# q and k of batches 1 to 7 transposed by DMA instead of by TensorE, in attention followed by a gated MLP

## The chip, the cores and the metric

The kernel runs on one core of one Trainium2 chip. The metric is the device time of one execution in microseconds, as a median of three runs. A core has five engines, each with its own instruction stream: TensorE (PE in the profile; its weight loads are PEld), VectorE (DVE), ScalarE (ACT), GpSimd (POOL) and SyncE (SP), which here only issues DMAs. Streams meet in semaphores. TensorE writes its results to PSUM, from which VectorE or ScalarE move them to SBUF. DMA transfers run on 16 DMA engines that all queues share.

## The reference

Eight batches, 16 query heads, 4 key/value heads, 384 positions, head size 64. Attention without a mask, then a gated MLP with a spatial mix over the positions:

```python
k = np.repeat(k, group, axis=1)              # group = 4
v = np.repeat(v, group, axis=1)
scores = scale * np.matmul(q, k.transpose(0, 1, 3, 2))
scores = scores - np.max(scores, axis=-1, keepdims=True)
attn = np.exp(scores)
attn = attn / (np.sum(attn, axis=-1, keepdims=True) + 1e-09)
x = np.matmul(attn, v)                        # then [B, S, 16 * 64] = [8, 384, 1024]

h = np.maximum(x @ w_in, 0.0)                 # [8, 384, 1024]
u, v = h[..., :512], h[..., 512:]
v_n = (v - mean(v)) / np.sqrt(var(v) + 1e-06)
v_s = np.einsum('ts,bsd->btd', w_spatial, v_n) + b_spatial[None, :, None]
out = (u * v_s) @ w_out                       # [8, 384, 1024], float32
```

Inputs and output are float32 in HBM. The kernel multiplies in fp16.

## The kernel before

**Layout.** A score matmul needs the head dimension on the partitions, for q and for k. HBM holds positions as rows, so q and k are loaded with 128 positions on the partitions (position 3p + t lies on partition p as piece t of three), cast to fp16, and transposed in blocks of 128x128: 128 positions by two heads of 64. A batch has 6 blocks of k (two pairs of heads, `gp`, times three pieces) and 24 of q (two `gp`, four heads `j` of a group, three pieces; the two heads of a block belong to the two kv heads of the pair). TensorE transposes them against an identity matrix into PSUM and VectorE copies them to SBUF: `transpose_k` makes one group of six blocks (PSUM tile `pk`, copied to `kT`), `transpose_q` one group of six (PSUM tile `pq_<gp>_<jp>`, copied to half of `qT_<gp>`). That is five groups a batch.

**Units of work.** A batch of attention has 18 score units (`scores`): two matmuls into a PSUM tile `sc` of two banks, of which there are two, and one exponential on ScalarE of 128x1024 into `aT`. Each `values` step (four a batch) runs 36 matmuls: sums of the exponentials (`sums`), of which ScalarE makes reciprocals by Ln and Exp (`rec`), and the products with v (`X`), which VectorE scales into `xT`. The MLP of a batch is a list of pieces: three `mk_v` (PSUM `pv`), four `mk_u` (`pu`), four `mk_sp` (`psp`) and six `mk_out` (`po`), with the layer norm on VectorE and ScalarE between. `sums`, `X`, `pv`, `pu`, `psp`, `po`, `pk`, `pq` and `psw` (the transposed spatial weights) share four PSUM buffers in turn, each of one bank.

**Order.** The streams of TensorE, GpSimd and SP stand in the order in which the program issues them; VectorE's and ScalarE's are scheduled by the compiler. A batch has nine visits of two score units. Behind the scores of a visit come, by visit: a `values` step (visits 0, 3, 5, 8; the one of visit 0 belongs to the batch before), a transpose group, and pieces of the MLP of the batch before, taken from a queue as long as the running sum of estimated times (`done`) is below a budget. The budget of a visit is a ninth of all estimates of a batch; a transpose group counts 0.36, and each piece its number in `feed_forward`. Transpose groups stand in visits 1 and 2 (second half of this batch's q: `pq_1_0`, `pq_1_1`) and 6, 7, 8 (next batch's k, first half of its q: `pk`, `pq_0_0`, `pq_0_1`). In batch 0 no MLP piece runs.

**Loads.** `load_batch(b + 1)` is called in visit 2 of batch b: k, first half of q, v, second half of q, all from SP into single float32 buffers, cast on GpSimd (for batch 1 k and the first half of q on VectorE). Output stores go through SP as well, one for each third of the positions (`osb`, three buffers). The MLP's weights are loaded and cast by DMAs that GpSimd issues in batch 0; the spatial weights (`ws`) come over SP.

Of the kernel before, what the change touches and what calls it, by code (L numbers as in the profile page):

```python
# [11 lines left out]
FP16 = mybir.dt.float16  # L12
# [6 lines left out]
def kernel(  # L19
# [19 lines left out]
    nc = tc.nc  # L39
    P = 128  # L40

    B, HQ, S, D = q.shape
    HKV = k.shape[1]
    G = HQ // HKV
# [3 lines left out]
    NST = S // P  # L48
    NKT = DM // P
    NDT = DH // P  # L50
    NGP = HKV // 2
# [10 lines left out]
    qk16 = ctx.enter_context(tc.tile_pool(name="qk16", bufs=2))  # L62
    tr_sb = ctx.enter_context(tc.tile_pool(name="tr_sb", bufs=3))
# [13 lines left out]
    for i, (_nm, funcs) in enumerate(get_activation_tables(nc.m.arch).items()):  # L77
        if need_funcs.issubset(funcs):
# [5 lines left out]
            name=nc.get_next_instruction_name(), act_func_set_id=set_id, ins=[], outs=[]  # L84
# [16 lines left out]
    def load_q(b, gp, pieces=1):  # L101
        q32 = ld.tile([P, 2 * G, NST * D], FP32, name=f"q32_{b}_{gp}", tag=f"q32_{gp}")
        n = 2 * G // pieces
        for i in range(pieces):
            h0 = gp * 2 * G + i * n
            nc.sync.dma_start(
                q32[:, i * n : (i + 1) * n, :],
                q[b, h0 : h0 + n].rearrange("h (p t) d -> p h (t d)", t=NST),
            )
        loaded["q32", b, gp] = q32  # L110

    def cast_k(b, engine):
        k16 = qk16.tile([P, NST, HKV, D], FP16, name=f"k16_{b}", tag="k16")
        engine.tensor_copy(k16, loaded["k32", b].rearrange("p g (t d) -> p t g d", t=NST))  # L114
        loaded["k16", b] = k16

    def cast_v(b, engine):
# [2 lines left out]
        loaded["v16", b] = v16  # L120

    def cast_q(b, gp, engine):
        q16 = qk16.tile([P, NST, G, 2, D], FP16, name=f"q16_{b}_{gp}", tag=f"q16_{gp}")
        q32 = loaded["q32", b, gp]
        for half in range(2):
            engine.tensor_copy(
                q16[:, :, :, half, :],
                q32[:, half * G : (half + 1) * G, :].rearrange("p j (t d) -> p t j d", t=NST),
            )
        loaded["q16", b, gp] = q16  # L130

# [82 lines left out]

    kT, qT, aT, xT = {}, {}, {}, {}

    def transpose_k(b):
        k16 = loaded[("k16", b)]
        pk = ps.tile([P, NGP, NST, P], FP16, name=f"pk_{b}", tag="ps")
        for gp in range(NGP):  # L220
            for t in range(NST):
                nc.tensor.transpose(  # L222
                    pk[:, gp, t, :],
                    k16[:, t, 2 * gp : 2 * gp + 2, :].rearrange("p g d -> p (g d)"),
                    ident16,
                )
        kT[b] = tr_sb.tile([P, NGP, NST, P], FP16, name=f"kT_{b}", tag="kT")
        nc.vector.tensor_copy(kT[b], pk)

    def transpose_q(b, gp, jp):  # L230
        q16 = loaded[("q16", b, gp)]
        if jp == 0:
            qT[b, gp] = tr_sb.tile([P, G, NST, P], FP16, name=f"qT_{b}_{gp}", tag=f"qT_{gp}", bufs=2)
        pq = ps.tile([P, 2, NST, P], FP16, name=f"pq_{b}_{gp}_{jp}", tag="ps")
        for jj in range(2):
            for t in range(NST):
                nc.tensor.transpose(
                    pq[:, jj, t, :],
                    q16[:, t, 2 * jp + jj, :, :].rearrange("p h d -> p (h d)"),
                    ident16,  # L240
                )
        nc.vector.tensor_copy(qT[b, gp][:, 2 * jp : 2 * jp + 2, :, :], pq)
# [169 lines left out]

    VISITS = 9
    VALUES_AT = {0: (-1, 1, 1), 3: (0, 0, 0), 5: (0, 0, 1), 8: (0, 1, 0)}
    T_SCORE, T_VALUES, T_TRANS = 0.62, 1.55, 0.36

    queue = []
    done = 0.0

    load_consts()  # L420
    with tc.manual_schedule(engines={PE, POOL, SP}):
        load_k(0)
        load_q(0, 0, pieces=2)
        cast_k(0, nc.vector)
        cast_q(0, 0, nc.vector)
        load_v(0)
        load_q(0, 1, pieces=2)
        cast_v(0, nc.gpsimd)
        cast_q(0, 1, nc.gpsimd)
        load_w_in(DH, DFF)  # L430
        load_w_in(0, DH)
        load_w_out()
        transpose_k(0)
        transpose_q(0, 0, 0)
        transpose_q(0, 0, 1)

        total = sum(t for t, _ in feed_forward(0))
        per_visit = (total + 4 * T_VALUES + 5 * T_TRANS) / VISITS
        budget = 0.0
        for b in range(B + 1):  # L440
            for vi in range(VISITS if b < B else 1):
                if b < B:
                    scores(b, [2 * vi, 2 * vi + 1])
                if vi in VALUES_AT:
                    db, gp, quad = VALUES_AT[vi]
                    if 0 <= b + db < B and (b < B or db < 0):
                        values(b + db, gp, quad)
                        done += T_VALUES
                if b < B:
                    if vi in (1, 2):  # L450
                        transpose_q(b, 1, vi - 1)
# [24 lines left out]
                if not queue:  # L476
                    done = max(done, budget - per_visit)
# [30 lines left out]
```

## Time and profile before

| | |
|---|---|
| median of 3 runs | 302.69 us (301.97 to 303.99) |
| the profiled execution | 303.19 us, span 301.4 us |
| TensorE busy | 269.2 us, 89% of the span, 2457 matmuls |
| ScalarE busy | 184.3 us, 61% |
| VectorE busy | 161.7 us, 54% |
| GpSimd busy | 53.2 us, 18% |
| mean granted TensorE clock | 0.980 |
| DMA | 35.57 MB in 31852 packets |

The profile is of one execution. Times are microseconds from the start of the span. A row of a timeline gives start, length, engine, line of the program, operation, output <- inputs, sizes and count, and in brackets how long the engine had been idle before it and what ended the wait. TensorE's matmuls overlap, so the length of a row is longer than the time by which it holds up the next one; differences of starts give that time. Tile names end in a running number of the program, which differs between the two kernels. The page leaves out the DMAs' issue from an engine's busy time; rows named SPq are issues on SP's queue.

### The profile page before, as it was taken

To read this page: it belongs to the slowest core of one execution; us is meant where nothing else is said; L and a number is where in the kernel's file an instruction comes from. 1 tells how busy PE (TensorE), PEld (TensorE's weight loads), DVE (VectorE), ACT (ScalarE), POOL (GpSimd) and SP (SyncE) were. 2 spreads that over 40 slices of the span, in tenths; PEclk is the share of its full clock that TensorE was granted. 3 is DMA by queue.
4 is the path that set the end of the run, shared out by engine and by line. 5 is a ranking of instruction groups with operands and counts; after the bars stand their busy time and mean duration, and the time that the engine had idled before them with its cause. 6 is when DMAs were issued, how large, how long until landed. Compare 5 with 4: busy or idle time off the path is not lost.

```text
span 301.4 us, 5836 instructions
## 1 busy us (share of the span) xinstructions
PE 269.2 (89%) x2457; PEld 125.4 (42%) x2457; DVE 161.7 (54%) x310; ACT 184.3 (61%) x249; POOL 53.2 (18%) x82
## 2 busy tenths in 40 slices
PE   0576879899899989999899989999899989999993
PEld 0332434444445434444345434444344434444551
DVE  3437325564465554665455654755455754645574
ACT  1396965657776585566786485566876485675300
POOL 0666952000140003200050001500051000000000
PEclk9977979999999999999999999999999999999998
DMA  7999991003660219103570219103480111003105
GB/s 216 315 287 218 116 254 35 2 0 142 197 188 2 119 52 318 37 0 141 164 222 0 103 50 316 56 2 140 137 251 0 70 73 72 0 2 139 72 0 209
DMA packets 31852, 35.57 MB, mean 118 GB/s; under 512 B 1489, under 2 KB 28114, under 8 KB 31826
## 3 DMA queue, kind: packets, MB, share of 16 engines
q1 hardware_dynamic: 28722, 32.05, 32.4%
q0 software_dynamic: 3104, 3.15, 6.8%
q8 instruction: 19, 0.31, 0.4%
q14 instruction: 7, 0.06, 0.1%
HBM read 25.76 MB, written 12.58 MB: 127 GB/s over the span
## 4 chain that ended last, share of the span: by engine, by line
PE 69%; ACT 16%; DMA 6%; DVE 4%; issue 2%; SPq 1%; POOL 0%; DVEq 0%
DMA ws_316<-in_moe_w_spatial_dram 3%; DMA q_0_1_135<-in_q_dram 3%; ACT aT_1_720 L265 1%; ACT aT_0_2385 L265 1%; ACT aT_0_969 L265 1%; ACT aT_1_335 L265 1%; ACT aT_0_1441 L265 1%; ACT aT_0_489 L265 1%; PE pv_0_588 L311 1%; ACT aT_0_3329 L265 1%; ACT aT_0_1913 L265 1%; ACT aT_0_2857 L265 1%; ACT aT_1_2613 L265 1%; ACT aT_1_3539 L265 1%; ACT aT_1_3085 L265 1%
## 5 line engine op out<-in xcount | busy, mean ns | idle before, releaser
L348 PEld LDWEIGHTS <-w_in_107 128*128 128x128 f16 x256 | 23.9, 98 | 21.6 <-issue 6.9
L186 POOL DMA_DIRECT2D w_in_107<-in_moe_w_in_dram x32 | 17.1, 543 | 5.3 <-DMA w_in_107<-in_moe_w_in_dram 5.3
L280 PEld LDWEIGHTS <-ones_103 128*32 128x32 f16 x384 | 7.4, 96 | 15.1 <-issue 13.3
L222 PE MATMUL pk_177<-ident_102,k_0_128 128*128 128x128 f16 x6 | 0.8, 303 | 9.6 <-DVE ident_102 L155 9.6
L265 ACT ACTIVATE aT_0_209<-sc_0_203 128x1024 f16<-128x1024 f32 x1 | 1.0, 1024 | 10.3 <-PE sc_0_203 L252 10.3
L114 POOL CAST k_3_1060<-k_3_1056 128x768 f16<-128x768 f32 x1 | 0.8, 827 | 33.0 <-DVE stats_0_1086 L321 33.0
L252 PEld LDWEIGHTS <-kT_184 64*128 64x128 f16 x36 | 2.1, 99 | 9.4 <-issue 8.9
L114 POOL CAST k_6_2476<-k_6_2472 128x768 f16<-128x768 f32 x1 | 0.8, 827 | 27.7 <-DMA k_6_2472<-in_k_dram 27.7
L114 POOL CAST k_5_2004<-k_5_2000 128x768 f16<-128x768 f32 x1 | 0.8, 827 | 26.6 <-DMA k_5_2000<-in_k_dram 26.6
L114 POOL CAST k_7_2948<-k_7_2944 128x768 f16<-128x768 f32 x1 | 0.8, 827 | 25.4 <-DMA k_7_2944<-in_k_dram 25.4
L114 POOL CAST k_4_1532<-k_4_1528 128x768 f16<-128x768 f32 x1 | 0.8, 827 | 25.1 <-DMA k_4_1528<-in_k_dram 25.1
L280 PEld LDWEIGHTS <-v_0_138 128*32 128x32 f16 x96 | 2.9, 106 | 4.4 <-issue 3.2
L202 DVE CAST ws_318<-ws_316 128x384 f16<-128x384 f32 x3 | 1.9, 671 | 5.2 <-DMA ws_316<-in_moe_w_spatial_dram 5.2
L222 PEld LDWEIGHTS <-k_0_128 128*128 128x128 f16 x6 | 0.6, 133 | 9.5 <-DVE k_0_128 L114 5.2
L364 PEld LDWEIGHTS <-bias_ones 128*128 128x128 f16 x32 | 3.1, 97 | 3.5 <-issue 2.3
L311 PEld LDWEIGHTS <-xt_271 128*128 128x128 f16 x24 | 2.7, 116 | 3.5 <-issue 1.6
L387 PEld LDWEIGHTS <-gT_3623 128*128 128x128 f16 x24 | 2.2, 98 | 3.5 <-issue 0.7
L387 PEld LDWEIGHTS <-gT_3895 128*128 128x128 f16 x24 | 2.3, 98 | 3.0 <-DVE gT_3895 L373 0.5
L387 PEld LDWEIGHTS <-gT_2697 128*128 128x128 f16 x24 | 2.2, 97 | 3.0 <-DVE gT_2697 L373 0.6
L387 PEld LDWEIGHTS <-gT_1753 128*128 128x128 f16 x24 | 2.2, 97 | 3.0 <-DVE gT_1753 L373 0.6
L387 PEld LDWEIGHTS <-gT_2225 128*128 128x128 f16 x24 | 2.2, 97 | 3.0 <-DVE gT_2225 L373 0.6
L387 PEld LDWEIGHTS <-gT_1281 128*128 128x128 f16 x24 | 2.2, 97 | 3.0 <-DVE gT_1281 L373 0.6
(1168 smaller groups left out, 804.7 us busy)
## 6 DMA issues: line engine op xcount, KB each, us to landing
w_in_107<-in_moe_w_in_dram POOLq DMA_DIRECT2D x32, 64.0 KB, 5.4
w_out_108<-in_moe_w_out_dram POOLq DMA_DIRECT2D x2, 512.0 KB, 7.4
q_0_0_125<-in_q_dram SPq DMA_DIRECT2D x2, 384.0 KB, 5.4
q_0_1_135<-in_q_dram SPq DMA_DIRECT2D x2, 384.0 KB, 8.3
q_1_0_247<-in_q_dram SPq DMA_DIRECT2D x1, 768.0 KB, 6.2
q_1_1_256<-in_q_dram SPq DMA_DIRECT2D x1, 768.0 KB, 8.5
q_2_0_571<-in_q_dram SPq DMA_DIRECT2D x1, 768.0 KB, 12.9
q_2_1_580<-in_q_dram SPq DMA_DIRECT2D x1, 768.0 KB, 8.2
```

Source lines behind the costliest of these rows:

```text
L114: engine.tensor_copy(k16, loaded["k32", b].rearrange("p g (t d) -> p t g d", t=NST))
L186: nc.gpsimd.dma_start(w_in16[32 * i : 32 * (i + 1), kc : kc + 2, c0:c1], rows[jq])
L202: nc.vector.tensor_copy(ws16[:, tt, :, :], ws32[:, tt, :].rearrange("p (s t) -> p t s", t=NST))
L222: nc.tensor.transpose(pk[:, gp, t, :], k16[:, t, 2 * gp : 2 * gp + 2, :].rearrange("p g d -> p (g d)"), ident16,)
L252: nc.tensor.matmul(sc[:, half, :], kT[b][lo:hi, gp, t, :], rhs[lo:hi, c * 512 : (c + 1) * 512], start=True, stop=True,)
L265: nc.scalar.activation(aT[b, gp][:, t, :, c * 512 : (c + 1) * 512], sc, AF.Exp, scale=scale)
L280: nc.tensor.matmul(dst[32 * i : 32 * (i + 1), 0:S], weights(t, half), a[:, t, half, j * S : (j + 1) * S], start=(t == 0), stop=(t == NST - 1),
L311: nc.tensor.matmul(pv, xt[:, kc, st * P : (st + 1) * P], w_in16[:, kc, DH:DFF], start=(kc == 0), stop=(kc == NKT - 1),)
L348: nc.tensor.matmul(pu[:, 0:S], w_in16[:, kc, mu * P : (mu + 1) * P], xT[b][:, kc, :], start=(kc == 0), stop=(kc == NKT - 1),)
L364: nc.tensor.matmul(psp[:, 0:S], bias_ones, bias_rows, start=True, stop=False)
L387: nc.tensor.matmul(po, gT[:, m, tt * P : (tt + 1) * P], w_out16[:, m, half * 512 : (half + 1) * 512], start=(m == 0), stop=(m == NDT - 1),)
```

## The change

The five TensorE groups stay for batch 0 alone. For each later batch three DMA transposes, issued on SP, move the fp16 tiles from SBUF to SBUF: all six blocks of k (`dma_transpose_k`), then twelve blocks of q, twice (`dma_transpose_q`). They write `kT` and `qT` directly, with no PSUM tile and no copy on VectorE. Batch b + 1's k and first half of q are issued in visit 6 of batch b, its second half of q in visit 8. The fp16 tiles get the layout in which the columns of a block lie side by side, so k is cast in two instructions of half the size. The estimate `T_TRANS` is gone from the budget, so the MLP's pieces fall on other visits.

```diff
     def cast_k(b, engine):
-        k16 = qk16.tile([P, NST, HKV, D], FP16, name=f"k16_{b}", tag="k16")
-        engine.tensor_copy(k16, loaded["k32", b].rearrange("p g (t d) -> p t g d", t=NST))
+        k16 = qk16.tile([P, NGP, NST, 2, D], FP16, name=f"k16_{b}", tag="k16")
+        k32 = loaded["k32", b].rearrange("p (gp h) (t d) -> p gp t h d", gp=NGP, t=NST)
+        for gp in range(NGP):
+            engine.tensor_copy(k16[:, gp], k32[:, gp])
...
+    def dma_transpose_k(b):
+        kT[b] = tr_sb.tile([P, NGP, NST, P], FP16, name=f"kT_{b}", tag="kT")
+        nc.sync.dma_start_transpose(
+            kT[b].rearrange("p g t q -> p (g t) q"),
+            loaded["k16", b].rearrange("p g t h d -> p (g t h d)"),
+        )
+
+    def dma_transpose_q(b, gp):
+        qT[b, gp] = tr_sb.tile([P, G, NST, P], FP16, name=f"qT_{b}_{gp}", tag=f"qT_{gp}", bufs=2)
+        nc.sync.dma_start_transpose(
+            qT[b, gp].rearrange("p j t q -> p (j t) q"),
+            loaded["q16", b, gp].rearrange("p j t h d -> p (j t h d)"),
+        )
...
-        per_visit = (total + 4 * T_VALUES + 5 * T_TRANS) / VISITS
+        per_visit = (total + 4 * T_VALUES) / VISITS
...
-                    if vi in (1, 2):
+                    if b == 0 and vi in (1, 2):
                         transpose_q(b, 1, vi - 1)
-                        done += T_TRANS
...
-                    if vi >= 6 and b + 1 < B:
-                        if vi == 6:
-                            transpose_k(b + 1)
-                        else:
-                            transpose_q(b + 1, 0, vi - 7)
-                        done += T_TRANS
+                    if vi == 6 and b + 1 < B:
+                        dma_transpose_k(b + 1)
+                        dma_transpose_q(b + 1, 0)
+                    if vi == 8 and b + 1 < B:
+                        dma_transpose_q(b + 1, 1)
```

How the order changes is shown at two places, for a batch in the middle. First SP's stream, from the loads of batch 4 to the loads of batch 5. Before:

```order
L93 DMA k_4_1528<-in_k_dram 128x4x192 [waits DMAHW3_49,DMAHW2_49,Pool_49]
L106 DMA q_4_0_1530<-in_q_dram 128x8x192 [waits DMAHW4_49,Pool_49]
L98 DMA v_4_1537<-in_v_dram 128x4x192 [waits DMAHW5_49,Pool_49]
L106 DMA q_4_1_1539<-in_q_dram 128x8x192 [waits DMAHW6_49,Pool_49]
L396 DMA out_dram<-osb_0_1795 128x1024 [waits DVE_49]
L396 DMA out_dram<-osb_1_1826 128x1024 [waits DMAHW7_49,DVE_49]
L396 DMA out_dram<-osb_2_1900 128x1024 [waits DMAHW0_49,DVE_49]
L93 DMA k_5_2000<-in_k_dram 128x4x192 [waits DMAHW2_49,DMAHW1_49,Pool_49]
```

And now:

```order
L93 DMA k_4_1421<-in_k_dram 128x4x192 [waits DMAHW3_49]
L106 DMA q_4_0_1423<-in_q_dram 128x8x192 [waits DMAHW4_49]
L98 DMA v_4_1431<-in_v_dram 128x4x192 [waits DMAHW5_49]
L106 DMA q_4_1_1433<-in_q_dram 128x8x192 [waits DMAHW6_49]
L221 DMA_TRANSPOSE kT_1655<-k_4_1425 128x6x128 [waits DMAHW7_49,Pool_49]
L228 DMA_TRANSPOSE qT_0_1657<-q_4_0_1428 128x12x128 [waits DMAHW0_49,PE_49,Pool_49]
L412 DMA out_dram<-osb_0_1692 128x1024 [waits DMAHW1_49,DVE_49]
L228 DMA_TRANSPOSE qT_1_1765<-q_4_1_1437 128x12x128 [waits DMAHW2_49,PE_49,Pool_49]
L412 DMA out_dram<-osb_1_1706 128x1024 [waits DMAHW3_49,DVE_49]
L412 DMA out_dram<-osb_2_1827 128x1024 [waits DMAHW4_49,DVE_49]
```

The two first transposes stand between the loads and the first output store, the third between the first store and the second. Each waits for a cast on GpSimd and for the DMA eight places earlier on SP (DMAHW).

Second VectorE's stream, where its rows show in which order TensorE's groups are drained from the last pieces of one batch to the layer norm in the next. Before:

```order
L394 COPY osb_1_1826<-po_1_0_1827 128x512 [waits DMAHW0_49,PE_49]
L394 COPY osb_1_1826<-po_1_1_1833 128x512 [waits PE_49]
L296 TENSOR_TENSOR xt_1606<-X_1_0_0_1864,rec_1_0_1861 128x384 [waits PE_49,Activation_49]
L296 TENSOR_TENSOR xt_1606<-X_1_0_1_1878,rec_1_0_1861 128x384 [waits PE_49]
L242 COPY qT_0_1810<-pq_0_1_1892 128x768 [waits PE_49]
L394 COPY osb_2_1900<-po_2_0_1901 128x512 [waits DMAHW1_49,PE_49]
L296 TENSOR_TENSOR xt_1606<-X_1_1_0_1932,rec_1_1_1929 128x384 [waits PE_49,Activation_49]
L296 TENSOR_TENSOR xt_1606<-X_1_1_1_1946,rec_1_1_1929 128x384 [waits PE_49]
L394 COPY osb_2_1900<-po_2_1_1960 128x512 [waits PE_49]
L242 COPY qT_1_1975<-pq_1_0_1976 128x768 [waits PE_49]
L242 COPY qT_1_1975<-pq_1_1_1992 128x768 [waits PE_49]
L321 BN_STATS stats_0_2030<-v_r_0_2028 128x6 [waits Activation_49]
```

And now:

```order
L410 COPY osb_1_1706<-po_1_0_1707 128x512 [waits DMAHW1_49,PE_49]
L312 TENSOR_TENSOR xt_1500<-X_1_0_0_1737,rec_1_0_1734 128x384 [waits PE_49,Activation_49]
L312 TENSOR_TENSOR xt_1500<-X_1_0_1_1751,rec_1_0_1734 128x384 [waits PE_49]
L410 COPY osb_1_1706<-po_1_1_1767 128x512 [waits PE_49]
L312 TENSOR_TENSOR xt_1500<-X_1_1_0_1799,rec_1_1_1796 128x384 [waits PE_49,Activation_49]
L312 TENSOR_TENSOR xt_1500<-X_1_1_1_1813,rec_1_1_1796 128x384 [waits PE_49]
L410 COPY osb_2_1827<-po_2_0_1828 128x512 [waits DMAHW2_49,PE_49]
L410 COPY osb_2_1827<-po_2_1_1834 128x512 [waits PE_49]
L337 BN_STATS stats_0_1888<-v_r_0_1886 128x6 [waits Activation_49]
```

The three `qT` copies and their TensorE groups are gone, and the output pieces moved: `po_1_1` now stands where `pq_0_1` stood, and `po_2_0` and `po_2_1` both follow the `values` step of the next batch's visit 0.

More of the change, by code (lines that the diff above doesn't have):

```diff
@@ L122, in cast_q @@
     def cast_q(b, gp, engine):
-        q16 = qk16.tile([P, NST, G, 2, D], FP16, name=f"q16_{b}_{gp}", tag=f"q16_{gp}")
+        q16 = qk16.tile([P, G, NST, 2, D], FP16, name=f"q16_{b}_{gp}", tag=f"q16_{gp}")
         q32 = loaded["q32", b, gp]
@@ L127, in cast_q @@
                 q16[:, :, :, half, :],
-                q32[:, half * G : (half + 1) * G, :].rearrange("p j (t d) -> p t j d", t=NST),
+                q32[:, half * G : (half + 1) * G, :].rearrange("p j (t d) -> p j t d", t=NST),
             )
@@ L223, in transpose_k @@
                     pk[:, gp, t, :],
-                    k16[:, t, 2 * gp : 2 * gp + 2, :].rearrange("p g d -> p (g d)"),
+                    k16[:, gp, t, :, :].rearrange("p h d -> p (h d)"),
                     ident16,
@@ L238, in transpose_q @@
                     pq[:, jj, t, :],
-                    q16[:, t, 2 * jp + jj, :, :].rearrange("p h d -> p (h d)"),
+                    q16[:, 2 * jp + jj, t, :, :].rearrange("p h d -> p (h d)"),
                     ident16,
@@ L414 @@
     VALUES_AT = {0: (-1, 1, 1), 3: (0, 0, 0), 5: (0, 0, 1), 8: (0, 1, 0)}
-    T_SCORE, T_VALUES, T_TRANS = 0.62, 1.55, 0.36
+    T_VALUES = 1.55
     queue = []
```

## The prediction

> **What bounds the kernel now.** I read the page's head first, then the busy time by stage, then TensorE's timeline across one boundary between batches, and last the DMA queues.
>
> The first fence is the page: span, TensorE's row, and the chain of work that ended last by engine.
>
> ```profile
> span 301.4 us, 5836 instructions
> PE 269.2 (89%) x2457; PEld 125.4 (42%) x2457; DVE 161.7 (54%) x310; ACT 184.3 (61%) x249; POOL 53.2 (18%) x82
> PE 69%; ACT 16%; DMA 6%; DVE 4%; issue 2%; SPq 1%; POOL 0%; DVEq 0%
> ```
>
> The second is busy time by stage: start and end, length, then each engine's busy time, granted clock, DMA share and GB/s.
>
> ```profile
> 12.00:30.00 18.00, 12.10 (x120) 4.88 (x117) 9.40 (x16) 14.21 (x18) 12.61 (x24) 0.82 1.09 268
> 30.00:42.00 12.00, 9.44 (x119) 4.68 (x119) 4.72 (x9) 11.88 (x15) 11.31 (x18) 0.93 1.00 147
> 113.00:147.30 34.30, 32.90 (x308) 15.15 (x306) 18.95 (x36) 22.91 (x33) 5.00 (x6) 1.00 0.36 117
> ```
>
> In the steady stage (113 to 147.3 us is one batch) TensorE is busy 32.9 of 34.3 us, ScalarE 22.9, VectorE 19.0, at a granted clock of 1.00; the DMA engines are in use for 0.36 of it, 12.3 us. So TensorE's instruction stream sets the batch time, and what leaves that stream shortens it, except where TensorE then waits for ScalarE. Before 42 us it is different: the DMA engines are full (shares 1.09 and 1.00), and ScalarE is busy 11.9 of 12 us.
>
> TensorE's timeline (start us, length us, instruction) shows both kinds of place. First the end of one batch and the start of the next; then the same places around batch 7, behind which no batch follows.
>
> ```profile
> 112.86 1.89 PE L311 MATMUL pv_0_1547<-w_in_107,xt_1134 128*128 128x512 f16 x8
> 137.70 0.67 PE L280 MATMUL sums_1_0_1848<-aT_1_1669,ones_103 128*32 128x384 f16 x12
> 139.28 0.51 PE L237 MATMUL pq_0_1_1892<-ident_102,q_4_0_1534 128*128 128x128 f16 x6
> 139.97 1.02 PE L387 MATMUL po_2_0_1901<-w_out_108,gT_1753 128*128 128x512 f16 x4 [0.18 <-ACT rec_1_0_1861 L291]
> 140.93 0.39 PE L252 MATMUL sc_0_1907<-qT_0_1810,kT_1775 64*128 64x512 f16 x2
> 144.55 0.51 PE L237 MATMUL pq_1_0_1976<-ident_102,q_4_1_1543 128*128 128x128 f16 x6
> 145.52 0.39 PE L252 MATMUL sc_4_1984<-qT_0_1810,kT_1775 64*128 64x512 f16 x2 [0.46 <-ACT aT_0_1913 L265]
> 146.44 0.39 PE L252 MATMUL sc_5_1987<-qT_0_1810,kT_1775 64*128 64x512 f16 x2 [0.52 <-ACT aT_0_1913 L265]
> 146.76 0.51 PE L237 MATMUL pq_1_1_1992<-ident_102,q_4_1_1543 128*128 128x128 f16 x6
> 147.10 1.24 PE L311 MATMUL pv_0_2019<-w_in_107,xt_1606 128*128 128x512 f16 x5
> ...
> 249.56 1.67 PE L311 MATMUL pv_0_3417<-w_in_107,xt_3022 128*128 128x512 f16 x7
> 273.27 0.67 PE L280 MATMUL sums_1_0_3700<-aT_1_3539,ones_103 128*32 128x384 f16 x12
> 274.85 1.04 PE L387 MATMUL po_2_0_3745<-w_out_108,gT_3623 128*128 128x512 f16 x4
> ```
>
> **The change part by part.**
>
> *Taken from TensorE: five groups of six transposes a batch.* One group keeps the stream 0.34 us (`pq_1_1` starts at 146.76, the next instruction at 147.10), not the 0.51 of its row, since matmuls overlap. What three of the groups cost can be read off directly, because batch 7 runs the same fillers without `pk`, `pq_0_0` and `pq_0_1`. From `pv_0` to `sums_1_0` batch 3 takes 137.70 − 112.86 = 24.84 us and batch 7 takes 273.27 − 249.56 = 23.71: 1.13 us for `pk` and `pq_0_0`. From `sums_1_0` to `po_2_0` it is 2.27 against 1.58: 0.69 us for `pq_0_1`, with the 0.18 us that `po_2_0` waited. Together 1.82 us.
>
> The other two stand among the scores of visits 1 and 2. `pq_1_0` lies in a stretch in which TensorE waits for a score buffer anyway; here are the two exponentials on ScalarE that it waits for:
>
> ```profile
> 144.44 1.02 ACT L265 ACTIVATE aT_0_1913<-sc_2_1967 128x1024 f16<-128x1024 f32 x1 [0.21 <-PE sc_2_1967 L252]
> 145.37 1.02 ACT L265 ACTIVATE aT_0_1913<-sc_3_1970 128x1024 f16<-128x1024 f32 x1
> ```
>
> `sc_4` starts when the first is done, with or without `pq_1_0` ahead of it; without, its wait grows from 0.46 to some 0.8 us. I count nothing. `pq_1_1` is behind the last of these waits and counts 0.34. So a batch gives 1.82 + 0.34 = 2.16 us. The lower bound takes the bare 0.34 for four groups, 1.36 us; the upper adds the gap that the other order may close (`po_0_0` then stands behind two scores and no longer right behind the product it needs; I allow 0.3), 2.5 us.
>
> This happens for batches 2 to 7, six times. Batch 1's `pk` and `pq_0` groups lie in the stage where ScalarE is full; they count nothing. Its `pq_1` groups:
>
> ```profile
> 35.05 0.39 PE L252 MATMUL sc_0_483<-qT_0_414,kT_404 64*128 64x512 f16 x2
> 40.60 0.82 PE L237 MATMUL pq_1_1_561<-ident_102,q_1_1_260 128*128 128x128 f16 x6
> 41.22 3.21 PE L311 MATMUL pv_0_588<-w_in_107,xt_271 128*128 128x512 f16 x8
> ```
>
> `pq_1_1` holds `pv_0` back by 0.62 us. Sum: 0.62 + 6 × 2.16 = 13.6 us (0.62 + 6 × 1.36 = 8.8 to 0.62 + 6 × 2.5 = 15.6).
>
> *Taken from VectorE:* five copies a batch out of PSUM, off the path with VectorE at 19 of 34 us; the four shared PSUM buffers turn over with fewer users. Counted at nothing. *The casts:* k is now cast in two halves and q in another layout; GpSimd casts for 5.0 us of 34.3, with the slack shown next, so nothing again.
>
> *Added to SP's queue: three DMA transposes a batch.* No row of before shows one, so its cost is bounded. A batch moves 30 blocks of 128x128 fp16, 0.98 MB, or 3840 rows of 256 bytes. The DMA queues (packets, MB, share of 16 engines):
>
> ```profile
> q1 hardware_dynamic: 28722, 32.05, 32.4%
> q0 software_dynamic: 3104, 3.15, 6.8%
> ```
>
> Queue 1 took 0.324 × 301.4 = 97.7 us for 32.05 MB, 328 GB/s: priced by bytes a batch's transposes take 3.0 us. A packet took 97.7 × 16 / 28722 = 54 ns: priced as one packet per row, 3840 × 54 / 16 = 13.1 us. A packet of queue 0 took 0.068 × 301.4 × 16 / 3104 = 106 ns: 25.3 us. I take 13.1, since the new transfers are issued on queue 1 too and their pieces are smaller than its 1.1 KB mean. The Trainium skill ("Advanced Engine Details and Errata", "X-Bar Transpose (TRN2)") says that a transposing DMA is as fast as a regular one; that is the byte price, and no row here shows it.
>
> With 12.3 us of other transfers the DMA engines are then used 25.4 us of a batch of 32.1. What hides it:
>
> ```profile
> 118.63 1.60 POOL L126 CAST q_4_0_1534<-q_4_0_1530 128x768 f16<-128x768 f32 x2 [1.58 <-PE sc_6_1598 L252]
> 136.26 0.36 SPq L396 DMA_DIRECT2D out_dram<-osb_0_1795  x1
> 145.92 0.33 SPq L396 DMA_DIRECT2D out_dram<-osb_2_1900  x1
> 156.13 0.38 PE L252 MATMUL sc_9_2137<-qT_1_1975,kT_1775 64*128 64x512 f16 x2
> ```
>
> The k and first q transposes wait on SP for GpSimd's casts, done at 120.2 (behind that wait on SP stands only the first output store, due 16 us later); the scores that read them start at 140.93, 20.7 us later. The second q transpose now stands behind the first output store (136.26) and is read by `sc_9` at 156.13, 19.5 us later. Behind it on SP are the other two stores, for which nobody waits soon (three output buffers), and the next loads, issued at 146 behind the third store and needed a batch later. If the cover is gone, each microsecond of lateness is a microsecond of TensorE.
>
> *Start.* Batch 1's transposes run while the DMA engines are full:
>
> ```profile
> 15.62 1.81 DVE L126 CAST q_1_0_251<-q_1_0_247 128x768 f16<-128x768 f32 x2 [1.45 <-DMA q_1_0_247<-in_q_dram]
> 23.53 1.85 DVE L202 CAST ws_318<-ws_316 128x384 f16<-128x384 f32 x3 [5.17 <-DMA ws_316<-in_moe_w_spatial_dram]
> 37.39 1.63 POOL L126 CAST q_1_1_260<-q_1_1_256 128x768 f16<-128x768 f32 x2
> ```
>
> They queue behind the spatial weights, landed at 23.5. Their 18 blocks take 7.9 us alone at the 54 ns price and 15.7 if the weight queue takes half: ready at 31 to 39, needed at 35.05. So 0 to 4 us late; I take 0, since batch 2's first loads, which stood in that place, now wait until 39 (behind the transpose that needs the cast at 37.39). Those loads are needed by `sc_0` of batch 2, a batch after 35.05.
>
> Against the profiled execution (303.19 us, a span of 301.4 and 1.8 around it; the median of the runs is 302.69, 0.5 lower): 303.2 − 13.6 = 289.6, and I say 289.5. Own range: 303.2 − 15.6 = 287.6 less the 0.5 to the median, 287, and 289.6 + 4.2 = 294.
>
> **The rivals.**
>
> *The DMA engines become the bound (slower).* Place: SP's queue, each batch. 32.1 − 12.3 = 19.8 us are free, so it decides from 19.8 × 16 / 3840 = 82 ns a row, between the two packet prices. At 106 ns a batch needs 12.3 + 25.3 = 37.6 us, 3.4 more than the 34.2 between the two `pv_0` of before (112.86 to 147.10): 303.2 + 6 × 3.4 = 323. The first sign would be `sc_0` waiting for a DMA. For it: nothing shows the price, and rows of 256 bytes are smaller than nearly all packets here. Against: the 54 ns packet, below the threshold, is that of the queue which will carry the transposes, and four times as large. The Trainium skill ("VectorE: DVE Perf Modes", "The three transpose paths") gives 1309 ns for one 128x128 block by DMA against 390 on TensorE, and its rules prefer TensorE where PSUM will do: were 30 blocks to add up, an estimated 39 us of transposing a batch and some 407 us in all. Chance 0.19.
>
> *The freed time comes back as waits.* If only `pq_0_0` and `pq_1_1` shorten a batch, because scores wait for exponentials where the groups stood, it is 0.62 + 6 × 0.68 = 4.7 us: 298.5. For it: `pq_1_0` already shows the case. Against: of the scores of batches 2 to 7 the list of waits names `sc_4` and `sc_5` alone, and the comparison with batch 7 is of whole stretches. Chance 0.14 (294 to 299.7).
>
> *More than counted:* all five groups at the 0.51 us of their rows and the closed gaps, 0.62 + 6 × 2.9 = 18 us, 285. Chance 0.03.
>
> That the change does not do what it says is excluded: the order of the new program has no transpose of batches 1 to 7 on TensorE.
>
> **How the numbers follow.** Forecast (287 to 294) 0.59, freed time lost 0.14, more 0.03, within 1% (299.7 to 305.7, about what a measurement can tell from no change) 0.05, DMA bound 0.19. Faster by over 1%: 0.76; within: 0.05; slower: 0.19. For 8 in 10 the range takes the forecast, the lost gain, the larger gain and part of the middle: 285.5 to 303.
>
> **What would show it.** Right: batches of about 32.1 us from `pv_0` to `pv_0`; TensorE's waits at `sc_4` grown to 0.8 us; no wait of `sc_0` or `sc_9` for a DMA; a DMA share of a batch of at most 0.8; batch 1's `sc_0` at about 35. Wrong: `sc_0` or `sc_9` waiting for `kT` or `qT`, SP issuing a transpose for many microseconds, or a batch still near 34 us with new waits for ScalarE or for a PSUM buffer.

## The result, and the profile after

| | before | after |
|---|---|---|
| median | 302.95 us (301.97 to 303.99) | 289.64 us (288.39 to 290.86) |
| ratio | | 0.956 (95% interval 0.9505 to 0.9615) |
| the profiled execution | 303.19 us, span 301.4 | 289.11 us, span 287.3 |

The medians are of four runs each. The kernel is 4.4% faster. The spans of the two profiled executions differ by 14.1 us.

The page of the kernel after, the rows that answer to those of before (TensorE and the other engines; the chain by engine; the DMA queues with packets, MB and share of 16 engines):

```profile
span 287.3 us, 5420 instructions
PE 255.2 (89%) x2247; PEld 113.3 (39%) x2247; DVE 143.8 (50%) x277; ACT 184.4 (64%) x249; POOL 54.0 (19%) x88
...
DMA packets 59402, 42.42 MB, mean 148 GB/s; under 512 B 29041, under 2 KB 55666, under 8 KB 59378
q1 hardware_dynamic: 56274, 38.94, 53.6%
...
PE 75%; ACT 11%; DMA 6%; DVE 4%; issue 1%; SPq 1%; POOL 0%
```

TensorE lost 14.0 us of busy time and the span 14.1, so its share stayed at 89%, and it carries more of the chain than before (75% against 69%). VectorE lost 17.9 us, most of it the copies out of PSUM. The DMA engines have 27550 packets and 6.85 MB more.

Busy time by stage, of the kernel after (start and end, length, busy time of PE, PEld, DVE, ACT and POOL, granted clock, DMA share, GB/s); the second row is a whole batch, from one `pv_0` to the next:

```profile
30.00:42.00 12.00, 9.52 (x95) 3.48 (x95) 2.14 (x4) 10.53 (x14) 10.63 (x19) 0.73 0.97 134
106.74:138.56 31.82, 30.40 (x278) 13.39 (x276) 16.14 (x31) 22.85 (x32) 4.93 (x7) 1.00 0.66 156
```

A batch is 31.82 us, with TensorE still busy for all but 1.4 of them, and the DMA engines used for 0.66 of it, up from 0.36. Where the batches begin shows how even the gain is. First TensorE's timeline of before, then the one of after, batches 2 to 5 and 1 to 5:

```profile
78.55 1.89 PE L311 MATMUL pv_0_1075<-w_in_107,xt_658 128*128 128x512 f16 x8
...
147.10 1.89 PE L311 MATMUL pv_0_2019<-w_in_107,xt_1606 128*128 128x512 f16 x8
181.02 1.89 PE L311 MATMUL pv_0_2491<-w_in_107,xt_2078 128*128 128x512 f16 x8
```

```profile
41.10 1.90 PE L327 MATMUL pv_0_554<-w_in_107,xt_273 128*128 128x512 f16 x8
74.61 1.90 PE L327 MATMUL pv_0_1005<-w_in_107,xt_624 128*128 128x512 f16 x8
106.74 1.90 PE L327 MATMUL pv_0_1441<-w_in_107,xt_1064 128*128 128x512 f16 x8
138.56 1.90 PE L327 MATMUL pv_0_1877<-w_in_107,xt_1500 128*128 128x512 f16 x8
170.39 1.90 PE L327 MATMUL pv_0_2313<-w_in_107,xt_1936 128*128 128x512 f16 x8
```

With the first `pv_0` of before at 41.22 the six intervals between one `pv_0` and the next are, in us:

| | 1 | 2 | 3 | 4 | 5 | 6 |
|---|---|---|---|---|---|---|
| before | 37.33 | 34.31 | 34.24 | 33.92 | 34.63 | 33.91 |
| after | 33.51 | 32.13 | 31.82 | 31.83 | 32.55 | 32.35 |

Intervals 2 to 6 gave 10.33 us together, 2.07 each; between the shortest of each kernel, called clean batches below, it is 33.91 − 31.82 = 2.09. Interval 1 gave 3.82, the stretch before it 0.12, and batch 7 nothing (28.79 and 28.83). That makes 14.2 us; behind the last `pv_0` the kernel after takes 0.1 us longer, which leaves the 14.1 of the spans.

At the boundary between two batches, TensorE and SP of the kernel after:

```profile
131.87 0.39 PE L268 MATMUL sc_0_1774<-qT_0_1657,kT_1655 64*128 64x512 f16 x2
...
137.32 0.39 PE L268 MATMUL sc_4_1849<-qT_0_1657,kT_1655 64*128 64x512 f16 x2 [0.90 <-ACT aT_0_1780 L281]
138.24 0.39 PE L268 MATMUL sc_5_1852<-qT_0_1657,kT_1655 64*128 64x512 f16 x2 [0.52 <-ACT aT_0_1780 L281]
```

```profile
111.28 2.00 SPq L221 DMA_TRANSPOSE kT_1655<-k_4_1425  x1
114.54 2.40 SPq L228 DMA_TRANSPOSE qT_0_1657<-q_4_0_1428  x1
128.75 0.36 SPq L412 DMA_DIRECT2D out_dram<-osb_0_1692  x1
129.21 3.38 SPq L228 DMA_TRANSPOSE qT_1_1765<-q_4_1_1437  x1
```

`sc_0` has no wait behind its row: `kT` and `qT_0` were issued 20.6 and 17.3 us before it. The only waits left in a clean batch are those of `sc_4` and `sc_5` for exponentials, 0.90 and 0.52 us. No score of the whole execution waits for a DMA.

### The profile page after: what moved, and what is told of

It reads as the page before. It is cut to its first block, busy times and chain, and to the rows that moved or that the text cites. A ratio compares the mean times of both kernels' runs of the same rounds, so it can differ in the third digit from the quotient of the medians.

```text
span 287.3 us, 5420 instructions
## 1 busy us (share of the span) xinstructions
PE 255.2 (89%) x2247; PEld 113.3 (39%) x2247; DVE 143.8 (50%) x277; ACT 184.4 (64%) x249; POOL 54.0 (19%) x88
## 4 chain that ended last, share of the span: by engine, by line
PE 75%; ACT 11%; DMA 6%; DVE 4%; issue 1%; SPq 1%; POOL 0%
DMA ws_318<-in_moe_w_spatial_dram 4%; DMA q_0_1_136<-in_q_dram 3%; ACT aT_1_337 L281 1%; ACT aT_0_2652 L281 1%; ACT aT_0_2216 L281 1%; ACT aT_0_471 L281 1%; ACT aT_0_1780 L281 1%; ACT aT_0_1344 L281 1%; ACT aT_0_3088 L281 1%; ACT aT_0_908 L281 1%; ACT aT_1_3288 L281 1%; ACT aT_1_686 L281 1%; SPq L106 1%; DVE ws_320 L204 1%; PE pv_0_3166 L327 1%
## 5 line engine op out<-in xcount | busy, mean ns | idle before, releaser
L364 PEld LDWEIGHTS <-w_in_107 128*128 128x128 f16 x256 | 23.4, 98 | 22.8 <-issue 8.8
L296 PEld LDWEIGHTS <-ones_103 128*32 128x32 f16 x384 | 7.4, 97 | 15.8 <-issue 14.1
L116 POOL CAST k_5_1861<-k_5_1857 128x384 f16<-128x384 f32 x2 | 1.0, 507 | 24.3 <-DMA k_5_1857<-in_k_dram 24.3
L116 POOL CAST k_6_2297<-k_6_2293 128x384 f16<-128x384 f32 x2 | 1.0, 507 | 24.1 <-DMA k_6_2293<-in_k_dram 24.1
L116 POOL CAST k_4_1425<-k_4_1421 128x384 f16<-128x384 f32 x2 | 1.0, 508 | 23.5 <-DMA k_4_1421<-in_k_dram 23.5
L116 POOL CAST k_7_2733<-k_7_2729 128x384 f16<-128x384 f32 x2 | 1.0, 508 | 23.4 <-DMA k_7_2729<-in_k_dram 23.4
L116 POOL CAST k_3_989<-k_3_985 128x384 f16<-128x384 f32 x2 | 1.0, 507 | 20.6 <-DVE mv_1004 L338 20.6
L238 PEld LDWEIGHTS <-k_0_128 128*128 128x128 f16 x6 | 0.6, 133 | 8.3 <-DVE k_0_128 L116 4.6
L312 DVE TENSOR_TENSOR xt_273<-X_1_0_0_435,rec_1_0_432 128x384 f16<-128x384 f32 x1 | 0.6, 558 | 6.5 <-ACT rec_1_0_432 L308 6.5
L327 PEld LDWEIGHTS <-xt_3225 128*128 128x128 f16 x24 | 2.4, 98 | 2.8
L403 PEld LDWEIGHTS <-gT_3644 128*128 128x128 f16 x24 | 2.3, 98 | 3.0 <-DVE gT_3644 L389 0.5
L327 PEld LDWEIGHTS <-xt_624 128*128 128x128 f16 x24 | 2.3, 98 | 2.8 <-issue 0.2
L327 PEld LDWEIGHTS <-xt_2808 128*128 128x128 f16 x24 | 2.3, 98 | 2.8 <-issue 0.2
L327 PEld LDWEIGHTS <-xt_2372 128*128 128x128 f16 x24 | 2.3, 98 | 2.8 <-issue 0.2
L327 PEld LDWEIGHTS <-xt_273 128*128 128x128 f16 x24 | 2.3, 98 | 2.8 <-issue 0.2
```

Source lines behind the costliest of these rows:

```text
L116: engine.tensor_copy(k16[:, gp], k32[:, gp])
L238: nc.tensor.transpose(pk[:, gp, t, :], k16[:, gp, t, :, :].rearrange("p h d -> p (h d)"), ident16,)
L296: nc.tensor.matmul(dst[32 * i : 32 * (i + 1), 0:S], weights(t, half), a[:, t, half, j * S : (j + 1) * S], start=(t == 0), stop=(t == NST - 1),
L327: nc.tensor.matmul(pv, xt[:, kc, st * P : (st + 1) * P], w_in16[:, kc, DH:DFF], start=(kc == 0), stop=(kc == NKT - 1),)
L364: nc.tensor.matmul(pu[:, 0:S], w_in16[:, kc, mu * P : (mu + 1) * P], xT[b][:, kc, :], start=(kc == 0), stop=(kc == NKT - 1),)
L403: nc.tensor.matmul(po, gT[:, m, tt * P : (tt + 1) * P], w_out16[:, m, half * 512 : (half + 1) * 512], start=(m == 0), stop=(m == NDT - 1),)
```

## The experiments

The theory: TensorE's stream got shorter by four groups a batch, `pq_1_0` had been free, a small part comes from the new order, and the DMA transposes cost nothing as long as they are issued early enough and the DMA engines have room. Against it stood: that the order gave the gain and not the groups; that the transposes cost something of their own, through contention, and hide a larger gain; and that the margin of the DMA engines is thin.

**Order alone.** The kernel before, with TensorE's groups, and with `T_TRANS` taken out of the planner's sums, so that the MLP's pieces fall on the visits they have after the change.

```diff
-        per_visit = (total + 4 * T_VALUES + 5 * T_TRANS) / VISITS
+        per_visit = (total + 4 * T_VALUES) / VISITS
...
-                        done += T_TRANS
```

> The kernel before with only the estimate of the transposes taken out of the budget: the MLP's pieces stand on the visits of the changed kernel, TensorE still transposes. My theory: the new order gives at most the gap behind the last spatial product, 0.3 us a batch, 300.5 to 303 us. The rival that the order is the gain: 290 to 295.

Measured: 299.95 us, ratio 0.9924 (0.9889 to 0.9958), a little faster than the 300.5 to 303 expected. A batch of it in busy time by stage:

```profile
111.49:145.00 33.51, 32.35 (x309) 15.13 (x307) 18.61 (x36) 22.86 (x32) 5.08 (x6) 1.00 0.37 119
```

A clean batch takes 33.51 us, 0.40 less than before and more than the 0.3 that was the most expected. Half of that can be seen in one place of before, where `po_0_0` stands right behind the last `psp`, whose product it reads by way of VectorE. It held the stream for 1.16 us (166.35 to 167.51 below); `po_2_0`, with as many matmuls and also followed by scores, held it for 0.96 (139.97 to 140.93). With the new order two scores and a group stand between, and `po_0_0` and the two pieces after it take 2.68 us, 0.89 each. TensorE's timeline of before at that place:

```profile
166.35 1.23 PE L387 MATMUL po_0_0_2268<-w_out_108,gT_2225 128*128 128x512 f16 x4
167.51 0.39 PE L252 MATMUL sc_14_2274<-qT_1_1975,kT_1775 64*128 64x512 f16 x2
```

The other 0.2 us I could not assign to an instruction. So the order alone is worth some 3 us, the groups the rest.

**Both.** The kernel after, with the five TensorE groups of each later batch put back in their visits; they write spare tiles that nothing reads (their copies on VectorE too), while the scores read what the DMAs wrote.

```diff
+                    if b > 0 and vi in (1, 2):
+                        spare_q(b, 1, vi - 1)
...
+                    if vi >= 6 and b + 1 < B:
+                        if vi == 6:
+                            spare_k(b + 1)
+                        else:
+                            spare_q(b + 1, 0, vi - 7)
```

> The changed kernel with the five TensorE groups and their VectorE copies of batches 1 to 7 put back, into a spare tile that nobody reads; the DMA transposes still feed the scores. My theory (the gain is TensorE's stream, the DMA is hidden): the time returns to that of the run with the new order and no DMA transposes, 300 to 304 us, and no score waits for a DMA. The rival that the DMA transposes cost something of their own, which the gain outweighs: 2 us or more above that run. The rival that the gain came from the order of the MLP's pieces: it stays below 295.

Measured: 302.91 us, ratio 0.9985 (0.9956 to 1.0014). The gain is gone once the groups are back. Beside the run above, which has the same groups in the same places and no DMA transposes, this one takes 3.0 us longer: the sign of the rival that the transposes cost something of their own. The intervals between the starts of `pv_0` say where. The shortest is 33.51 us in both, and intervals 2 to 6 have a mean of 33.79 us against 33.67, so a steady batch pays nothing or some 0.1 us. The rest is in the start: the first `pv_0` stands at 44.31 us against 42.66, and interval 1 takes 36.70 us against 35.32. TensorE's timeline of this kernel:

```profile
41.98 0.82 PE L276 MATMUL pq<-ident,q 128*128 128x128 f16 x6 [4.87 <-POOL q L128]
```

And of the one with the order alone:

```profile
41.34 0.51 PE L237 MATMUL pq<-ident,q 128*128 128x128 f16 x6 [1.89 <-POOL q L126]
```

Batch 1's `pq_1_0` waits for GpSimd's cast of q in both. The longer wait is not a later cast in the main: the group starts 0.6 us later, but TensorE had come to it 2.3 us earlier (the scores ahead of it start at 36.41 us, against 38.75). Behind the longer wait the matmuls run slower (rows of 0.82 us instead of 0.51), and the granted clock from 42 to 50 us is 0.68, against 1.00. Whether the transposes cause this is not shown: GpSimd casts when it has issued the weights' loads, and the last of these issues starts at 38.12 us here, at 37.47 in the run above, at 37.34 in the kernel after and at 35.19 in the one before, so it moves without DMA transposes too. The 3.0 us are measured; their cause in the start stays open. The kernel after has no instruction on TensorE that waits for that cast.

**One group.** The kernel before, with `pq_1_0` alone replaced by a DMA transpose of half a q tile (issued in visit 8). q is cast in the layout of the change; the order and the budget are those of before.

```diff
-                        transpose_q(b, 1, vi - 1)
+                        if b == 0 or vi == 2:
+                            transpose_q(b, 1, vi - 1)
...
+                    if vi == 8 and b + 1 < B:
+                        dma_transpose_half(b + 1)
```

> The kernel before with one group alone, pq_1_0, moved to a DMA transpose of half a q tile; everything else, the order and the budget too, as before. My theory (this group filled a wait for ScalarE): sc_4 waits some 0.8 us instead of 0.46 and the batch keeps its 34.2 us; 301.5 to 303. The rival that each group counts 0.34 us: 6 x 0.34 = 2.0 us less, 300.5 to 301, with batches of 33.9.

Measured: 303.29 us, ratio 1.0007 (0.9967 to 1.0046); a clean batch takes 33.91 us, as before; the 33.9 that the rival named is thus no sign of it. TensorE's timeline where the group stood:

```profile
143.71 0.39 PE L259 MATMUL sc<-qT,kT 64*128 64x512 f16 x2 [0.90 <-ACT aT L272]
144.62 0.39 PE L259 MATMUL sc<-qT,kT 64*128 64x512 f16 x2 [0.52 <-ACT aT L272]
```

The wait ahead of `sc_4` grew from 0.46 to 0.90 us and took up all of the removed group. A fifth of the groups was worth nothing.

**The DMA work twice and four times.** The kernel after, with each DMA transpose followed by one more, or by three more, of the same source into spare tiles.

```diff
+        for i in range(1):      # range(3) in the other
+            more = tr_sb.tile([P, NGP, NST, P], FP16, name=f"mk_{b}_{i}", tag="more_k", bufs=2)
+            nc.sync.dma_start_transpose(
+                more.rearrange("p g t q -> p (g t) q"),
+                loaded["k16", b].rearrange("p g t h d -> p (g t h d)"),
+            )
...
```

> The changed kernel with each DMA transpose issued twice, the second into a spare tile. In the profile after, the transposes take some 8.6 us of the DMA engines a batch. My theory (cover left): 8.6 more of a batch of 31.8, of which 21 are used, so within 1% of the changed kernel, 288 to 292. The rival that the transposes were just covered: each batch longer by several us, 300 or more.

> The changed kernel with each DMA transpose issued four times, three of them into spare tiles. Two issues left the time as it was, and the DMA share of a batch went from 21 us (once) to 27 (twice) of 32. The theory (hidden while the transfers of a batch fit into a batch) expects 27 + 2 x 5.5 = 38 us of transfers a batch and so batches of 36 to 40 us, 315 to 340 us in all, with scores that wait for a DMA. The rival that these transfers never reach TensorE: 288 to 292.

Measured: twice 289.24 us, ratio 0.9569 (0.9529 to 0.961), no different from the change itself; four times 311.62 us, ratio 1.0294 (1.0219 to 1.0368), a little less than expected. A batch with twice the transposes:

```profile
107.41:139.23 31.82, 30.40 (x278) 13.40 (x277) 16.14 (x31) 22.86 (x32) 4.94 (x7) 1.00 0.83 187
```

Two batches with four times, and the scores' wait of that kernel (total us, times, longest):

```profile
117.20:155.40 38.20, 32.97 (x279) 14.04 (x277) 16.40 (x31) 22.86 (x32) 4.92 (x7) 0.91 1.09 234
155.40:187.20 31.80, 30.38 (x278) 13.40 (x276) 16.14 (x31) 22.83 (x32) 4.93 (x7) 1.00 1.08 236
```

```profile
PE sc L280 <- DMA qT<-q: 15.3, 6, 4.5
```

The second copy takes the DMA engines' time from 0.66 × 31.82 = 21.0 to 0.83 × 31.82 = 26.4 us a batch, and TensorE's batch stays at 31.82. With four the share is over 1 in both batches shown, transposes fall behind, scores wait for `qT`, and some batches pay for it: interval 1 takes 40.95 us, intervals 2 to 6 take 33.19, 38.2, 31.82, 36.51 and 32.88, 34.5 in the mean. So the prediction's rival exists, but between two and four times the work of the change.

**Later.** The kernel after, with k and the first half of q issued in visit 8 instead of visit 6. Nothing else is changed.

```diff
-                    if vi == 6 and b + 1 < B:
+                    if vi == 8 and b + 1 < B:
                         dma_transpose_k(b + 1)
                         dma_transpose_q(b + 1, 0)
```

> The changed kernel with the transposes of k and of the first half of q issued in visit 8 instead of 6, so behind the first output store, some 3 us before the first score that reads them (sc_0) and no longer 17 to 20 us. The theory (only the distance hides them) expects sc_0 of batches 2 to 7 to wait 2 to 6 us each for a DMA: 6 x 2 to 6 x 6 more, 301 to 326 us. The rival that a transpose lands within 2 us of its issue and needs no cover: below 294.

Measured: 316.11 us, ratio 1.0442 (1.0381 to 1.0503). The same transposes, issued two visits later, turn 4.4% of gain into 4.4% of loss. SP's queue, TensorE's timeline at that place, and the kernel's list of waits:

```profile
137.08 1.51 SPq L221 DMA_TRANSPOSE kT<-k  x1
138.70 4.21 SPq L228 DMA_TRANSPOSE qT<-q  x2
```

```profile
143.49 0.61 PE L268 MATMUL sc<-qT,kT 64*128 64x512 f16 x4 [3.67 <-DMA qT<-q]
144.02 0.83 PE L296 MATMUL sums<-aT,ones 128*32 128x384 f16 x12
144.63 2.14 PE L296 MATMUL X<-aT,v 128*32 128x384 f16 x24
...
150.57 0.39 PE L268 MATMUL sc<-qT,kT 64*128 64x512 f16 x2 [0.90 <-ACT aT L281]
```

```profile
PE sc L268 <- DMA qT<-q: 17.9, 6, 3.7
```

From the issue of `kT` to the first score it is 6.4 us, which is what needs to be hidden; the change hides it in 20.6. Six waits are 17.9 us, but the run is 26.5 us slower than the change: 4.4 us for a wait of 3.0 in the mean. Most of the rest is the clock. Busy time by stage during one wait and behind it:

```profile
140.00:143.40 3.40, 0.00 (x0) 0.00 (x0) 1.62 (x3) 0.00 (x0) 0.00 (x0) 1.00 0.84 179
143.40:146.50 3.10, 3.01 (x40) 1.31 (x40) 0.00 (x0) 2.55 (x4) 0.00 (x0) 0.66 0.86 251
146.50:149.50 3.00, 3.00 (x16) 1.03 (x13) 2.04 (x4) 0.29 (x1) 0.00 (x0) 0.78 0.00 0
```

Behind this wait the granted clock is 0.66 and then 0.78 for some 6 us. From the first score to `sc_4` it takes 7.08 us (143.49 to 150.57) against 5.45 in the change (131.87 to 137.32): 1.6 us on top of the wait of 3.67. All six waits of this trace, with the granted clock of the 5 us behind each and the time from `sc_0` to the next `pv_0` (6.69 us in the change, 131.87 to 138.56):

| `sc_0` at, us | 70.44 | 105.45 | 143.49 | 181.23 | 217.54 | 252.85 |
|---|---|---|---|---|---|---|
| wait, us | 2.78 | 2.69 | 3.67 | 3.24 | 2.78 | 2.71 |
| clock | 1.00 | 0.66 | 0.66 | 0.66 | 1.00 | 0.66 |
| `sc_0` to `pv_0`, us | 6.70 | 8.33 | 8.32 | 8.33 | 6.70 | 8.33 |

Where the clock falls, the stretch takes 1.63 us more; where it doesn't, nothing. The length of the wait alone does not decide it here: 2.69 and 2.71 us lowered the clock, 2.78 us twice did not. The waits and four times 1.63 us are 24.4 of the 26.5 us.

**A better order.** What is left to gain in a batch of the change is TensorE's wait at `sc_4` and `sc_5`, 1.42 us. Work of the MLP may stand there if its queue is filled in visit 1 instead of visit 2. The second version fills only part of the gap, by holding `po_2_1` back from visit 0 to visit 1; the third is the kernel before with the order of the first and TensorE's groups, so that the worth of the DMA transposes is seen in that order as well.

```diff
-                    if vi == 2 and b > 0 or b == B:
+                    if vi == 1 and b > 0 or b == B:
```

```diff
                 while queue and (b == B or done < budget):
+                    if vi == 0 and b < B and len(queue) == 1:
+                        break
```

> The changed kernel with the MLP pieces of the batch before queued from visit 1 instead of 2, so that the first pieces (pv) stand between the scores sc_2, sc_3 and sc_4, sc_5, where TensorE waits 0.9 + 0.52 us a batch for ScalarE. The theory (TensorE's stream bounds the batch, and this wait is its largest gap) expects 0.5 to 1.4 us less a batch, seven times: 280 to 286 us. The rival that the wait moves to pv, whose input is finished behind the same exponentials: 288 to 292.

> The changed kernel with the last output piece (po_2_1) held back from visit 0 to visit 1, into the same gap: it keeps TensorE 0.87 us. The theory expects the wait at sc_4 gone but for a rest and 0.87 us less a batch, six times: 283 to 286. The rival that the gap is ScalarE's and stays, whatever stands in it: 288 to 292.

> The kernel before, TensorE transposing all batches, with the two changes of order alone: the estimate of the transposes out of the budget, and the MLP pieces queued from visit 1. With pv in the gap between sc_3 and sc_4 no group of transposes fills a wait any more. The theory (a group keeps the stream 0.34 us wherever TensorE doesn't wait) expects five groups to count: a batch of 30.69 + 5 x 0.34 = 32.4 us and 280.5 + 6 x 1.7 + 0.3 = 291 us, so the DMA transposes are still worth some 10 us. The rival that the groups are absorbed once the gap is filled: below 286. The rival that the better order needs the DMA transposes: above 297.

Measured: 280.49 us, ratio 0.9241 (0.9186 to 0.9296); 285.71 us, 0.9454 (0.9413 to 0.9495); 294.78 us, 0.9724 (0.969 to 0.9758). A stretch of 31 us of the first, a little more than its batch of 30.69:

```profile
78.00:109.00 31.00, 30.93 (x280) 13.42 (x279) 16.69 (x31) 23.14 (x32) 5.48 (x8) 1.00 0.68 165
```

TensorE is busy for 30.93 of 31.00 us, and the batch got shorter by 31.82 − 30.69 = 1.13 us. This version beats both kernels. In this order the DMA transposes are worth 294.78 − 280.49 = 14.3 us; a batch with groups takes 32.95, so a group costs (32.95 − 30.69) / 5 = 0.45 us, with the waits it causes, now that none of the five is swallowed by a wait. Those batches are also why it is over the expected 291: I had them at 32.4, and six times 0.55 is 3.3 of the 3.8 us. The second version was to fill the gap with one piece of 0.87 us and gained 0.34 to 0.48 in its clean batches (31.34 to 31.48): `pu` then waits for VectorE five times, 2.8 us in all, which the change had twice, for 0.9 us in all. In these five batches the three `v_n` of the layer norm take 2.0 to 3.0 us together, beside casts on GpSimd, where they take 1.46 without.

## Why the prediction was right

The time (289.5 predicted, 289.64 measured) and the mechanism were right, and so were the signs: batches of 32.1 us in the mean, `sc_4` waiting 0.90 us, no score waiting for a DMA, a DMA share of 0.66, batch 1's `sc_0` at 35.37. Three sizes in the sum were not, the groups, the order and the start. The first two nearly cancelled (six times 0.47 us too much, six times 0.40 too little), so that agreement to 0.2 us is luck. (The 4.2 us in the upper end of the range have no working; the sum's own lower bound of 8.8 us gives 294.4.)

**The groups and the order.** The sum had 2.16 us a batch from the groups and nothing from the order, with 0.3 as its upper bound. Measured on clean batches: 33.91 (before) to 33.51 (order alone) to 31.82 (groups gone as well), so 0.40 from the order and 1.69 from the groups, 2.09 in all. The term that was too large is the 1.13 us for `pk` and `pq_0_0`, read from batch 3 against batch 7. Batch 3 was not a clean batch. Here is where it lost 0.33 us, then the same place in batch 4, both from the kernel before:

```profile
122.20 1.81 POOL L126 CAST q_4_1_1543<-q_4_1_1539 128x768 f16<-128x768 f32 x2 [1.20 <-PE sc_8_1662 L252]
122.28 1.05 DVE L330 TENSOR_SCALAR v_n_2_1596<-v_r_2_1584,mv_1546,rstd_1589 128x512 f16<-128x512 f32 x1
123.84 1.46 PE L348 MATMUL pu_2_1681<-xt_1134,w_in_107 128*128 128x384 f16 x8 [0.17 <-DVE xt_1606 L296]
...
156.51 0.54 DVE L330 TENSOR_SCALAR v_n_2_2068<-v_r_2_2056,mv_2018,rstd_2061 128x512 f16<-128x512 f32 x1
156.81 1.70 POOL L126 CAST q_5_1_2015<-q_5_1_2011 128x768 f16<-128x768 f32 x2 [1.17 <-DMA q_5_1_2011<-in_q_dram]
157.75 1.46 PE L348 MATMUL pu_2_2153<-xt_1606,w_in_107 128*128 128x384 f16 x8
...
171.62 0.67 PE L280 MATMUL sums_1_0_2320<-aT_1_2141,ones_103 128*32 128x384 f16 x12
```

`pu_2` waited for VectorE, which took twice as long for `v_n_2`, an instruction that ran beside a cast on GpSimd. This is what sets the longer batches apart in these two traces: a `v_n` that overlaps a cast for 0.7 us or more took 0.74 to 1.12 us, every other 0.53 to 0.55, and such slow rows stand in intervals 2, 3 and 5 before and 2, 5 and 6 after, the ones longer than the clean ones. So the longer batches go with the moment at which a load lands and its cast starts; that the cast is the cause is not tested. With batch 4 the same comparison gives (171.62 − 147.10) − 23.71 = 0.81 us instead of 1.13, and 0.81 + 0.69 + 0.34 = 1.84 for the groups. Part of what is left above 1.69 may be the gap at `po_0_0`, which batch 4 has and which belongs to the order. The 0.18 us in which `po_2_0` waited was rightly inside the 0.69: it is gone in the change and still there in the run with the order alone.

**`pq_1_0`** was counted at nothing, with the wait of `sc_4` growing to 0.8 us. It grew to 0.90, and the run that removes this group alone gained nothing. The rival in which the freed time comes back as waits thus described one group of five; none of the others had a wait behind it.

**The start.** The term of 0.62 us for batch 1 was mis-sized and came in another place: `pv_0` starts only 0.12 us earlier, but interval 1 gave 3.82 us, 1.7 more than a steady one. In the kernel before, `pv_0` took 3.21 us there, in the change 1.90. The stages of that place, first before, then after:

```profile
41.20:44.00 2.80, 2.80 (x10) 1.08 (x8) 0.56 (x1) 0.81 (x1) 0.11 (x1) 0.52 1.08 274
```

```profile
41.00:44.00 3.00, 3.00 (x16) 1.37 (x15) 0.34 (x1) 2.15 (x3) 0.15 (x1) 1.00 1.09 189
```

The clock was 0.52 there before and 1.00 now, while in the stage from 30 to 42 us it is lower now (0.73 against 0.93). I took the clock in the start as given. That the change moved it is not shown, because it differs between executions in which TensorE has been given the same work: up to the first `pv_0` the kernel before and the run with the order alone issue the same instructions on TensorE. Their stages from 30 to 36 us, before first:

```profile
30.00:36.00 6.00, 4.98 (x73) 2.42 (x73) 1.65 (x4) 5.91 (x8) 6.00 (x12) 0.98 0.94 119
```

```profile
30.00:36.00 6.00, 5.70 (x50) 2.17 (x47) 1.44 (x3) 5.28 (x7) 5.38 (x11) 0.50 0.78 101
```

The second `pv_0` starts at 78.55 us before, at 77.98 with the order alone and at 74.61 with the change, so up to there the order gave 0.6 us and the rest 3.4, where the sum had 0.62 + 2.16 = 2.8. With single executions this split is rough: interval 1 takes 37.33 us before, 35.32 with the order alone and 36.02 with one group gone, so the 1.7 us that it gave beyond a steady one may be chance of the execution profiled.

**The price of a DMA transpose.** A batch was to take 13.1 us of the DMA engines, between 3.0 and 25.3. The packets came out as thought, one for each row of 256 bytes (queue 1 has 27552 more, for 7 × 3840 = 26880 rows). Queue 1 took 0.536 × 287.3 − 0.324 × 301.4 = 56.3 us more; if its other transfers cost what they did before, a packet took 56.3 × 16 / 27552 = 33 ns, not 54, and a batch 8.0 us. The shares of a batch (0.66 of 31.82 us against 0.36 of 34.3) give 8.7 us. That made the margin larger than argued, and it was larger still than this price says, since a second copy added 5.4 us. By bytes, as the Trainium skill has it ("Advanced Engine Details and Errata", "X-Bar Transpose (TRN2)"), it would have been an estimated 3.0 us, which the runs don't show. The 1309 ns that the Trainium skill gives for a block ("VectorE: DVE Perf Modes", "The three transpose paths") don't add up either: 30 blocks took 8.7 us in all. The rule of the Trainium skill on the same page ("Rules for kernel authors"), to use TensorE where PSUM will do, is not borne out here, where TensorE's stream is the bound: following it costs 4.4%.

**What hides them.** 20.7 us of cover were counted for k and the first half of q; the issues stand 20.6 and 17.3 us ahead of `sc_0`, and 6.4 are needed. "If the cover is gone, each microsecond of lateness is a microsecond of TensorE" was too mild: 3.0 us of waiting cost 4.4 in the mean, since in four of six cases the clock fell behind the wait.

**The DMA bound as a rival** had its threshold at 19.8 us of transposes a batch. Twice the work (14.1 us above the other transfers) is free, four times (some 26 us) is not. The chance of 0.19 was spent on a case that needed more than twice the price measured.

## What to carry to other kernels

Where one engine's stream sets the time, look for work on it that another unit can do, and price each piece at its place: four groups of transposes gave their time and the fifth, which stood in a wait, gave none until the order was changed as well. Time a piece by comparing stretches with and without it, but on several batches, and take the shortest; a single disturbed batch had put 0.3 us into the estimate. The same holds for the start: what one execution shows of it before another is not yet the change. A transfer that takes over such work is free only if it is issued long enough ahead, so measure the distance in the trace and move the issue, not only the work.

## What the runs showed of the hardware

- The transposing DMAs from SBUF to SBUF moved about one packet per row of 256 bytes (27552 for 26880 rows), at 33 ns a packet, where ordinary transfers on the same queue took 54 ns for 1.1 KB. The second copy of the same data cost less than the first (5.4 against 8.7 us a batch); why, the runs don't show.
- SP was held by the issue of such a transpose for 1.8 to 3.5 us (k, 768 columns) and 1.7 to 3.4 us (half of q, 1536 columns) in the kernel after from 50 us on, against 0.4 to 1.0 for a load, and longest where the DMA engines are full, in its start:

```profile
15.92 7.84 SPq L228 DMA_TRANSPOSE qT_0_401<-q_1_0_253  x1
```

- Waits of 2.69 to 3.67 us on TensorE were followed, in four cases of six, by a granted clock of 0.66 over 5 us, which cost 1.6 us on top of the wait. The Trainium skill ("TensorE: Matmul & The Clock Gate", "Why this matters for your kernels") asks for no gap over about 3 us; the trace agrees for 3.24 and 3.67 us, but 2.69 and 2.71 lowered the clock too, and 2.78 twice did not.
- The layer norm's `v_n` on VectorE (SBUF to SBUF) took 0.74 to 1.12 us instead of 0.54 wherever it overlapped a cast on GpSimd for 0.7 us or more, in both kernels. The VectorE instructions of the same stretches that read PSUM (`uT`, `xT`) kept their 0.54 to 0.56 us beside a cast, and `BN_STATS` its 0.69. The cause is not tested.
